# Turning v, r and a by rearranged DRAM copies and 32x32 blocks on VectorE in a fused RWKV-7 and MoE kernel

## The chip, the cores and the metric

The kernel runs on one core of a Trainium2 chip. The metric is device time in microseconds (us) for one execution; before the change it was 804.31 us, the median of 3 runs (802.88 to 806.55). The engines are named TensorE (PE in the profile, PEld for its weight loads), VectorE (DVE), ScalarE (ACT), POOL and SyncE (SP, whose queue is SPq). SyncE issues nearly all DMAs.

## The reference

Two blocks follow each other. The first is a recurrence over 768 steps, for 4 batches and 8 heads of 40 columns, with a 40x40 state per head:

```python
for t in range(S):
    kt, vt, rt = (k[:, :, t], v[:, :, t], r[:, :, t])
    wt, at, bt = (w[:, :, t], a[:, :, t], b[:, :, t])
    y[:, :, t] = np.einsum('bhd,bhde->bhe', rt, state)
    Sa = np.einsum('bhde,bhe->bhd', state, at)
    state_decay = state * wt[:, :, None, :] - np.einsum('bhd,bhe->bhde', Sa, bt)
    state = state_decay + np.einsum('bhd,bhe->bhde', vt, kt)
```

y is laid out as 3072 tokens of 320 columns, x, and the second block computes `h = x @ w_in; g = h * np.cos(h); out = g @ w_out` with d_ff = 2048. All of it is float32 on the chip; the MoE weights arrive as float64 words and are rounded there.

## The kernel before

**Chunks.** The sequence is cut into 24 chunks of C = 32 steps. A tile holds one chunk of one tensor with (batch, step) on the 128 partitions and (head, column) along the free side: 32 partitions a batch. Columns are padded from 40 to DP = 64 where pairs of heads are turned together. Each chunk's recurrence is rewritten as matrix products: Gram matrices between steps, a triangular inverse (made for four chunks at a time, mostly on VectorE), and the state carried from chunk to chunk.

**Turning.** These products need a tile's columns on the partitions. `turned` (L327) does it with four TensorE transposes of 128x128, each taking two heads: the result has (head parity, column up to 64) on the partitions and (pair of heads, batch, step) along the free side.
- v and r: `p2_in` (L584) copies the natural tiles nat_v and nat_r to the padded tiles vp and rp on POOL, with the heads reordered so that each transpose takes heads j and j + 4. `p2_v` (L604) turns both into one PSUM tile (eight transposes), and ScalarE copies the halves to vT and rT.
- a: `p1_a` (L406) works on two chunks at a time. From chunk 4 on it turns both (eight transposes), and `a_W` (L399) on VectorE multiplies the PSUM result by the cumulative decays wx into aT.
- w, k and b (scaled) are turned in the same way.

PSUM tiles for all of this come from `at` (L324), two in rotation.

**The recurrence of a chunk** is `ch_t`, `ch_q`, `ch_x`, `ch_s`, `ch_z` (states turned, products, result yt). `tokens` (L771) sends yt through a DRAM tile xd and back into xT, the MoE's input, 256 tokens for two chunks. The MoE is cut into pieces (`first_a`, `first_b`, `second`), 16 for each pair of chunks. A pair's pieces may begin with the chunk after the pair.

**Order.** The order is written out by hand at the end (from L1049): for each chunk a list of segments, with M where one MoE piece goes. The letters are t, q, x, s, z for the chain of chunk c; v, k, g for `p2_v`, `p2_k`, `p2_g` of chunk c + 1; pw, pa, pb, pn for w, a, b and the products of later chunks. `step` (L346) runs a segment; `later(n, work)` puts work, mostly loads, behind the n-th step from there. Every engine runs its instructions in this program order. Chunk 2 has 18 segments, chunk 3 has 25. `landed` (L597) has the next chunk's k, v and r loaded when both users of this one's have run. In the program the DMAs of SyncE use eight semaphores in turn, and each waits for the DMA eight places before it.

**Loads.** `load` (L146) fetches one tensor of a chunk with four DMAs, one for each batch, of 32 x 8 rows of 40 floats (160 bytes). `ws_fetch`, `ws_scan` and `ws_store` (L159 to L178) make the cumulative products of w, four chunks at a time, and keep them in a DRAM tile wd, from which w is loaded from chunk 4 on. During chunks 0 to 3 the same queue also fetches the MoE weights (words).

Of the kernel before, what the change touches and what calls it, by code (L numbers as in the profile page):

```python
# [9 lines left out]
F32 = mybir.dt.float32  # L10
I32 = mybir.dt.int32
U32 = mybir.dt.uint32
ALU = mybir.AluOpType
# [7 lines left out]
def kernel(  # L21
# [43 lines left out]
    nc = tc.nc  # L65
    B, H, S, D = r.shape
    P, C, DP = 128, 32, 64
    HH = H // 2
    NCH = S // C
# [5 lines left out]
    blk = [slice(C * i, C * i + C) for i in range(4)]  # L75
# [5 lines left out]
    ring = ctx.enter_context(tc.tile_pool(name="ring", bufs=7))  # L81
    sb1 = ctx.enter_context(tc.tile_pool(name="sb1", bufs=1))
    sb2 = ctx.enter_context(tc.tile_pool(name="sb2", bufs=2))
    sb3 = ctx.enter_context(tc.tile_pool(name="sb3", bufs=3))
    dram = ctx.enter_context(tc.tile_pool(name="dram", bufs=2, space=bass.MemoryType.DRAM))
# [4 lines left out]
    def kept(name, shape, n=1, fill=None, part=lambda t: t, on=nc.gpsimd):  # L90

        tiles = []
        for i in range(n):
            t = const.tile(shape, F32, tag=f"{name}{i}", name=f"{name}{i}")
            if fill is not None:
                on.memset(part(t), fill)
            tiles.append(t)
        return tiles
# [8 lines left out]
    src = {"r": r, "k": k, "v": v, "w": w, "a": a, "b": b}  # L107
# [11 lines left out]
    nat = {}  # L119
    for n, fill in (("w", 1.0), ("a", 0.0), ("b", 0.0)):  # L120
        for i in range(4):
            x = slice((i - 2) * H * DP, (i - 1) * H * DP)
            if i < 2:
                t = const.tile([P, H, DP], F32, tag=f"nat_{n}{i}", name=f"nat_{n}{i}")
            else:
                t = {
                    "w": w_in_sb[:, 0, late:], "a": w_in_sb[:, 1, late:], "b": late_out
                }[n][:, x].rearrange("p (h d) -> p h d", h=H)
# [4 lines left out]
    for n in "kvr":  # L133
        t = const.tile([P, H, D], F32, tag=f"nat_{n}", name=f"nat_{n}")
# [3 lines left out]
    vp, rp = (kept(n, [P, H, DP], 1, 0.0, padding, nc.vector)[0] for n in ("vp", "rp"))  # L138
# [4 lines left out]
    NZ = 2 * (C + DP) - DP + D  # L143
    qz = kept("qz", [P, B, 2, NZ], 1, 0.0, on=nc.vector)[0]

    def load(c, names, via=nc.sync, parts=range(B)):  # L146
        for n in names:
            for i in parts:
                at_c = src[n][i, :, c * C : (c + 1) * C, :]
                if n == "w" and c >= 4:  # L150
                    at_c = wd[c // 4][i, :, c % 4]
                via.dma_start(nat[n, c][blk[i], :, :D], at_c.rearrange("h t d -> t h d"))  # L152
# [171 lines left out]
    def at(name):  # L324
        return ps_a.tile([P, 2, 512], F32, tag="at", name=name)

    def turned(ps, x):  # L327

        for i in range(4):
            nc.tensor.transpose(  # L330
                ps[:, i * P : (i + 1) * P], x[:, 2 * i : 2 * i + 2].rearrange("p e d -> p (e d)"), ident
            )

    flat = lambda t: t.rearrange("p q t -> p (q t)")
    b4 = lambda t: t.rearrange("p (q t) -> p q t", t=C)
    unpad = lambda t: t[:, :, :D]
    G = {"rest": []}
# [5 lines left out]
    def later(steps, work):  # L343
        waiting.append([steps, work])

    def step(work, of_inv=0, of_w=0, small=False):  # L346


        before = list(waiting)
        work()  # L350
        G["small"] = small and G["kind"]
        for w in before:
            w[0] -= 1
            if w[0] == 0:
                waiting.remove(w)
                w[1]()
        for steps, n in ((inv_steps, of_inv), (w_steps, of_w)):
            for _ in range(min(n, len(steps))):
                steps.pop(0)()
# [29 lines left out]
    def from_one(c):  # L389

        nc.gpsimd.memset(G["wb", c][:, : 4 * P : C], 1.0)

    def over_w(c, wn):
        rw = ring.tile([P, H, D], F32, tag="rw", name="rw")
        nc.vector.reciprocal(rw, wn)  # L395
        nc.gpsimd.tensor_tensor(unpad(bn_b[c % 7]), unpad(nat["b", c]), rw, ALU.mult)  # L396
        G["rw", c] = rw

    def a_W(c, aps):  # L399
        aT = ring.tile([P, 4, P], F32, tag="aT", name="aT")  # L400
        nc.vector.tensor_tensor(
            aT.rearrange("p j (b t) -> p (j b) t", b=B), b4(aps), G["wx", c], ALU.mult
        )
        G["aT", c] = aT

    def p1_a(c):  # L406
        if c >= 4:
            ps = at("aps")
            for i in range(2):
                turned(ps[:, i], nat["a", c + i])  # L410
            for i in range(2):
                a_W(c + i, ps[:, i])
            over_w(c + 1, unpad(nat["w", c + 1]))
            return
        for c in range(c, c + 2):
            wn = ps_h.tile([P, 512], F32, tag="h", name="wn")
            aps = ps_o.tile([P, 512], F32, tag="o", name="aps")
            for j in range(4):
                nc.tensor.transpose(
                    wn[:, j * P : (j + 1) * P], G["wb", c][:, j * P + 1 : (j + 1) * P + 1], ident  # L420
                )
            from_one(c)
            turned(aps, nat["a", c])
            over_w(c, unpad(wn.rearrange("p (h d) -> p h d", h=H)))
            a_W(c, aps)
# [156 lines left out]


    def p2_in(c):  # L584
        for dst, m in ((vp, "v"), (rp, "r")):
            nc.gpsimd.tensor_copy(  # L586
                dst.rearrange("p (i f) d -> p f i d", f=2)[:, :, :, :D],
                nat[m, c].rearrange("p (f i) d -> p f i d", f=2),
            )
        landed(c)  # L590

    def p2_kn(c):
        nc.gpsimd.tensor_tensor(unpad(kn_b[c % 2]), nat["k", c], G["rw", c], ALU.mult)
        nc.gpsimd.tensor_copy(vvm[c % 2][:, :, C : C + D], nat["v", c])
        landed(c)

    def landed(c):  # L597

        G["users", c] = G.get(("users", c), 0) + 1
        if G["users", c] == 2 and c + 1 < NCH:  # L600
            for i, n in enumerate("kvr"):
                later(3 + i if c > 1 else 1, lambda n=n: load(c + 1, n))

    def p2_v(c):  # L604
        ps = at("vT")
        turned(ps[:, 0], vp)
        turned(ps[:, 1], rp)
        G["vT"] = sb3.tile([P, 4, P], F32, tag="opT", name="vT")
        G["rT", c] = sb2.tile([P, 4, P], F32, tag="rT", name="rT")
        nc.scalar.copy(G["vT"].rearrange("p j t -> p (j t)"), ps[:, 0])  # L610
        nc.scalar.copy(G["rT", c].rearrange("p j t -> p (j t)"), ps[:, 1])
# [38 lines left out]
    def ch_t(c):  # L650
        ps = at("sT")
        G["s"] = sb1.tile([P, 2 * B, P], F32, tag="s", name="s")
        for i in range(2 * B):
            nc.tensor.transpose(  # L654
                ps[:, i // 4, (i % 4) * P : (i % 4 + 1) * P], qz[:, i // 2, i % 2, C : C + P], ident
            )
        for i in range(2):
            nc.scalar.copy(G["s"][:, 4 * i : 4 * i + 4].rearrange("p i e -> p (i e)"), ps[:, i])  # L658

    def ch_q(c):  # L660
        ps = at("qps")
        for i in range(2 * B):
            for e in range(2):
                for f in range(2):
                    mm(
                        ps[half[e], f, i * C : (i + 1) * C], G["s"][half[f], i, half[e]],
                        G["rT", c][half[f], 2 * (i % 2) + e, blk[i // 2]], i == 0,
                    )
        for rows in half:
            nc.scalar.copy(  # L670
                pick(qz[rows], 0, (NZ - C, 2), (NZ, 2 * B), (1, C)),
                ps[rows, :, : 2 * B * C].rearrange("p f (i t) -> p f i t", t=C),
            )
# [247 lines left out]
    def main(c):  # L921
        def last():
            ch_z(c)
            if c + 2 < NCH:
                later(8 if c == 2 else 1, lambda: p2_kn(c + 2))

        return [lambda: ch_t(c), lambda: ch_q(c), lambda: ch_x(c), lambda: ch_s(c), last]

    with tc.manual_schedule():
# [64 lines left out]
        for seg in (other[1], *first[2:], *other[2:]):  # L994
            step(seg)
        scanned(1)
        p2_in(0)
        p2_kn(0)
        inv_space()
        inv_steps.extend(by_blocks(0))  # L1000
        v, k, g = p2(0)
# [44 lines left out]
        seconds = [lambda n=n: pair_second(0, n, n > 2) for n in range(4)]  # L1046
        (F1, F2, F3), (S1, S2, S3) = firsts[1:], seconds[1:]
        FILL = {(1, 6): 6, (1, 9): 14, (2, 0): 6, (2, 3): 6, (2, 5): 4, (2, 11): 29, (3, 3): 13, (3, 4): 20}
        for c in range(NCH):  # L1049
            t, q, x, s, z = main(c)  # L1050
            v, k, g = p2(c + 1) if c + 1 < NCH else [lambda: None] * 3
            q0 = c - c % 4 + 4
# [49 lines left out]
            n = len(segs)  # L1102
# [9 lines left out]
            for i, seg in enumerate(segs):  # L1112
                kept_busy(FILL.get((c, i), 0))
                while seg is s and ("rt", c) not in G:
# [57 lines left out]
```

## Time and profile before

| what | value |
|---|---|
| median of 3 runs | 804.31 us (802.88 to 806.55) |
| span of the profiled execution, first to last instruction | 803.7 us |
| what lies around the span, taken as median less span | 0.6 us |
| mean granted TensorE clock | 0.973 |
| DMA packets on SyncE's queue q1 | 177440, 52.11 MB |
| eight transposes of v and r (171.87 us in the chain) | 1.67 us |
| chunk 2 / 3 / 4 / 5 / 6 begins at | 90.8 / 127.5 / 169.9 / 206.5 / 245.0 us |

The profiled execution's own time is not listed apart from its span, so sums are made against the span and set beside the median. The profile lists busy time of each engine, the chain of work that ended last (each step followed back to what released it), groups of instructions with their mean duration, and each DMA queue with its packets. A chunk's place is told by the first transposes of the state (sT).

### The profile page before, as it was taken

The numbers are of one execution on the slowest core, as the hardware profiler recorded it, in microseconds if no ns is written. First come the engines' busy times: TensorE is split into PE (matmuls) and PEld (weight loads), VectorE is DVE, ScalarE is ACT, GpSimd is POOL, SyncE is SP. The second block draws the span as 40 slices with busy tenths as digits, with TensorE's granted clock in tenths as the row PEclk, the third lists the DMA queues.
The fourth block names the chain that finished last, engine by engine and source line by source line (L and its number), as shares of the span: only waits on it lengthen the run. The fifth ranks groups of instructions, "written<-read, shape, count | busy, mean of one in ns | idle before, by whom it ended". The sixth has DMA issues, their size and how long they took to land.

```text
span 803.7 us, 39602 instructions
## 1 busy us (share of the span) xinstructions
PE 753.0 (94%) x17812; PEld 578.6 (72%) x17812; DVE 487.9 (61%) x1025; ACT 387.2 (48%) x723; POOL 200.2 (25%) x354
## 2 busy tenths in 40 slices
PE   4777799999989999999999999999999999999997
PEld 4545577777767777777777787777787777777775
DVE  8879858854634796553895644994346863333231
ACT  1337766554434436545435635534645445354352
POOL 5326634320321220330330230332031122201000
PEclk9778999999999999999999999999999999999999
DMA  8675462443253324334224314223220222001000
GB/s 113 164 187 141 132 171 64 91 93 66 50 122 55 71 40 68 68 99 69 54 44 68 91 40 69 52 44 71 45 46 21 46 46 53 20 16 34 20 17 16
DMA packets 183304, 55.79 MB, mean 69 GB/s; under 512 B 157152, under 2 KB 178656, under 8 KB 183136
## 3 DMA queue, kind: packets, MB, share of 16 engines
q1 hardware_dynamic: 177440, 52.11, 30.1%
q8 instruction: 140, 2.29, 1.2%
q10 hardware_dynamic: 5440, 0.82, 0.7%
q0 software_dynamic: 256, 0.33, 0.3%
q14 instruction: 28, 0.23, 0.1%
HBM read 42.07 MB, written 11.14 MB: 66 GB/s over the span
## 4 chain that ended last, share of the span: by engine, by line
PE 68%; DVE 14%; ACT 5%; DMA 5%; issue 4%; POOL 2%; SPq 2%; DVEq 0%; ACTq 0%; POOLq 0%
PE ph L101 24%; PE po L101 20%; PE x0ps L101 4%; PE dps L101 3%; DVE rw L395 3%; PE gram L101 3%; PE vT L330 3%; PE sps L101 2%; DVE inv_tmp L494 2%; DVE inv L498 2%; PE nps L101 2%; PE qps L101 2%; PE sT L654 1%; SPq L152 1%; PE kT L330 1%
## 5 line engine op out<-in xcount | busy, mean ns | idle before, releaser
L101 PE MATMUL po<-w_out_sb,gT 128*128 128x320 f32 x768 | 223.3, 439 | 0.0
L101 PE MATMUL ph<-xT,w_in_sb 128*128 128x256 f32 x768 | 187.8, 389 | 1.9 <-issue 1.9
L101 PEld LDWEIGHTS po<-w_out_sb,gT 128*128 128x128 f32 x768 | 140.1, 190 | 54.4 <-issue 2.0
L101 PEld LDWEIGHTS ph<-xT,w_in_sb 128*128 128x128 f32 x768 | 140.8, 192 | 31.9 <-issue 14.1
L829 ACT ACTIVATE turns<-ph,rnd 128x512 f32<-128x512 f32 x96 | 64.2, 685 | 159.9 <-PE ph L101 159.5
L831 DVE SCALAR_TENSOR_TENSOR turns<-turns,ph 128x512 f32<-128x512 f32 x96 | 64.1, 683 | 115.3 <-ACT turns L829 115.0
L839 DVE TENSOR_TENSOR gT<-ph,turns 128x512 f32<-128x512 f32 x96 | 65.7, 686 | 39.1 <-ACT turns L836 39.1
L755 POOL TENSOR_TENSOR qz<-qz,wc 128x160 f32<-128x160 f32 x92 | 42.1, 475 | 167.5 <-DVE qz L754 166.8
L836 ACT ACTIVATE turns<-turns,half_pi 128x512 f32<-128x512 f32 x96 | 69.3, 722 | 3.1
L835 ACT ACTIVATE turns<-turns 128x512 f32<-128x512 f32 x96 | 60.2, 627 | 18.9 <-DVE turns L831 18.9
L101 PE MATMUL ph<-xT,w_in_tail 64*128 64x256 f32 (+1 forms) x512 | 55.0, 393 | 2.7 <-issue 2.7
L498 DVE TENSOR_TENSOR inv<-inv,inv_tmp 128x31 f32<-128x31 f32 (+15 forms) x124 | 50.7, 409 | 4.3
L754 DVE TENSOR_TENSOR qz<-dps,qz 128x160 f32<-128x160 f32 x92 | 28.9, 314 | 35.5 <-PE dps L101 35.4
L586 POOL COPY vp<-nat_v 128x320 f32<-128x320 f32 x24 | 12.0, 500 | 153.7 <-DMA nat_v<-in_v_dram 133.1
L494 DVE TENSOR_TENSOR inv_tmp<-u,inv 128x31 f32<-128x31 f32 (+15 forms) x124 | 48.3, 390 | 2.3
L395 DVE RECIPROCAL rw<-nat_w 128x320 f32<-128x320 f32 x20 | 42.8, 2141 | 0.1
L658 ACT COPY s<-sT 128x512 f32<-128x512 f32 x46 | 24.5, 583 | 35.9 <-PE sT L654 35.9
L101 PEld LDWEIGHTS ph<-xT,w_in_tail 64*128 64x128 f32 (+1 forms) x512 | 32.2, 160 | 12.2 <-issue 8.6
L766 POOL TENSOR_TENSOR yt<-yt,wb 128x512 f32<-128x512 f32 x24 | 31.6, 1316 | 22.3 <-DVE yt L761 22.3
L396 POOL TENSOR_TENSOR bn<-nat_b,rw 128x320 f32<-128x320 f32 x22 | 19.9, 906 | 43.9 <-DVE rw L395 37.1
L642 ACT COPY vvm<-gram 128x256 f32<-128x256 f32 x24 | 8.8, 368 | 45.6 <-DVE ag L637 45.2
L718 DVE TENSOR_TENSOR sm<-sps,su 128x128 f32<-128x128 f32 x48 | 11.7, 284 | 31.1 <-ACT sm L713 28.4
(136 smaller groups left out, 1130.6 us busy)
## 6 DMA issues: line engine op xcount, KB each, us to landing
words<-in_moe_w_in_dram SPq DMA_DIRECT2D x8, 512.0 KB
xd<-yt SPq DMA_DIRECT2D x48, 80.0 KB
out_dram<-ot SPq DMA_DIRECT2D x24, 160.0 KB
nat_k<-in_k_dram SPq DMA_DIRECT2D x92, 40.0 KB
nat_v<-in_v_dram SPq DMA_DIRECT2D x92, 40.0 KB
nat_r<-in_r_dram SPq DMA_DIRECT2D x92, 40.0 KB
nat_a<-in_a_dram SPq DMA_DIRECT2D x84, 40.0 KB
ws<-in_w_dram SPq DMA_DIRECT2D x5, 640.0 KB
```

The costliest lines, as they stand in the source:

```text
L101: nc.tensor.matmul(o, lhsT=lhsT, rhs=rhs, start=start, stop=stop, skip_group_check=True)
L330: nc.tensor.transpose(ps[:, i * P : (i + 1) * P], x[:, 2 * i : 2 * i + 2].rearrange("p e d -> p (e d)"), ident)
L395: nc.vector.reciprocal(rw, wn)
L494: nc.vector.tensor_tensor(tmp, u[:, j : j + 1, :j].to_broadcast([P, C - j, j]), x[:, j:, j : j + 1].to_broadcast([P, C - j, j]), ALU.mult,)
L498: nc.vector.tensor_tensor(x[:, j:, :j], x[:, j:, :j], tmp, ALU.subtract)
L755: nc.gpsimd.tensor_tensor(z, z, wc.rearrange("p (f m b) -> p f m b", f=2, m=2)[:, :, :, bb] .unsqueeze(3).to_broadcast([P, 2, 2, D]), ALU. ...
L766: nc.gpsimd.tensor_tensor(yt.rearrange("p j b t -> p (j b) t"), yt.rearrange("p j b t -> p (j b) t"), wx, ALU.mult)
L829: nc.scalar.activation(n, u, ACTF.Identity, bias=rnd, scale=1.0)
L831: nc.vector.scalar_tensor_tensor(n, n, -ROUND, u, ALU.add, ALU.subtract)
L835: nc.scalar.activation(n, n, ACTF.Abs)
L836: nc.scalar.activation(n, n, ACTF.Sin, bias=half_pi, scale=-2.0 * math.pi)
L839: nc.vector.tensor_tensor(gT[:, 2 * e : 2 * e + 2].rearrange("p f t -> p (f t)"), us[e], ns[e], ALU.mult)
```

## The change

v and r from chunk 6 on, and a from chunk 8 on, take another way.
- `spread` copies a range of chunks of one tensor from its DRAM input into a new DRAM tile, with one DMA for each head and each half of 32 columns: the tile's layout is [head group e, column half y, step, j, batch, 32 columns]. There are 16 copies for each of six ranges: a for chunks 8 to 12, v and r for 6 to 12, then v, r and a for 12 to 24. The second half reads columns 32 to 64, so it runs into the next step's row (those columns are not used); for the last head of the last range the last row is copied apart, to stay inside the tensor, which makes that copy 383 rows.
- The 96 copies wait in a list. `step` issues up to `G["rate"]` of them behind each segment: 2 in chunks 2 and 3, 1 from chunk 4 on.
- `load_turned` fetches a chunk with four DMAs of 32 rows of 2 KB: partitions then hold (e, y, step).
- `by_block` turns the tile with one VectorE instruction that transposes every 32x32 block. No PSUM tile is used. v and r go straight to vT and rT; a goes to aT and POOL multiplies it there by the decays.
- r is no longer loaded in the natural layout from chunk 6 on, a from chunk 8 on. v still is, since `p2_kn` copies it into vvm.

```diff
+    TURNED = {"v": 6, "r": 6, "a": 8}
+    apart, copies = {}, []
+
+    def spread(n, lo, hi):
+        x = src[n]
+        rows = (hi - lo) * C
+        to = dram.tile([2, 2, rows, HH, B, C], F32, tag=f"{n}t{lo}", name=f"{n}t")
+        for c in range(lo, hi):
+            apart[n, c] = to[:, :, (c - lo) * C : (c - lo + 1) * C]
+
+        def copy(h, y):
+            e, j = (h % 2, h // 2) if n == "a" else (h // HH, h % HH)
+            at = x.offset + h * S * D + lo * C * D
+            last = y == 1 and h == H - 1 and hi == NCH
+            parts = [(0, rows - last, 0, y * C, C)]
+            if last:
+                parts += [(rows - 1, rows, 0, C, D - C), (rows - 1, rows, D - C, 0, 2 * C - D)]
+            for r0, r1, o, d, m in parts:
+                nc.sync.dma_start(
+                    to[e, y, r0:r1, j, :, o : o + m],
+                    bass.AP(x.tensor, at + r0 * D + d, [[D, r1 - r0], [H * S * D, B], [1, m]]),
+                )
+
+        return [lambda h=h, y=y: copy(h, y) for h in range(H) for y in range(2)]
+
+    def load_turned(c, n, t):
+        for q in range(4):
+            nc.sync.dma_start(
+                t[blk[q]].rearrange("p h d -> p (h d)"),
+                apart[n, c][q // 2, q % 2].rearrange("t j b d -> t (j b d)"),
+            )
...
+    def by_block(to, x):
+        nc.vector.transpose(to.rearrange("p j t -> p (j t)"), x.rearrange("p h d -> p (h d)"))
...
         work()
+        for _ in range(min(G.get("rate", 0), len(copies))):
+            copies.pop(0)()
...
     def p1_a(c):
+        if c >= TURNED["a"]:
+            for i in range(2):
+                aT = ring.tile([P, 4, P], F32, tag="aT", name="aT")
+                by_block(aT, nat["a", c + i])
+                at_q = aT.rearrange("p j (b t) -> p (j b) t", b=B)
+                nc.gpsimd.tensor_tensor(at_q, at_q, G["wx", c + i], ALU.mult)
+                G["aT", c + i] = aT
+            over_w(c + 1, unpad(nat["w", c + 1]))
+            return
...
     def p2_in(c):
+        if c >= TURNED["v"]:
+            load_turned(c, "v", vp)
+            load_turned(c, "r", rp)
+            landed(c)
+            return
...
-            for i, n in enumerate("kvr"):
-                later(3 + i if c > 1 else 1, lambda n=n: load(c + 1, n))
+            for i, n in enumerate("kvr" if c + 1 < TURNED["v"] else "kv"):
+                later(3 + i if c > 1 else 1, lambda n=n: natural(c + 1, n))
...
     def p2_v(c):
+        if c >= TURNED["v"]:
+            G["vT"] = sb3.tile([P, 4, P], F32, tag="opT", name="vT")
+            G["rT", c] = sb2.tile([P, 4, P], F32, tag="rT", name="rT")
+            by_block(G["vT"], vp)
+            by_block(G["rT", c], rp)
+            return
...
+        for n, lo, hi in (
+            ("a", 8, 12), ("v", 6, 12), ("r", 6, 12), ("v", 12, NCH), ("r", 12, NCH), ("a", 12, NCH)
+        ):
+            copies.extend(spread(n, lo, hi))
         for c in range(NCH):
+            G["rate"] = {2: 2, 3: 2}.get(c, 1 if c > 3 else 0)
```

## The prediction

> **What bounds the kernel now.** I read the page's chain and engine table first, then busy time by stretch, then SyncE's own timeline and the chain around 170 us, because the change works through SyncE's queue.
>
> ```profile
> span 803.7 us, 39602 instructions
> PE 753.0 (94%) x17812; PEld 578.6 (72%) x17812; DVE 487.9 (61%) x1025; ACT 387.2 (48%) x723; POOL 200.2 (25%) x354
> ...
> PE 68%; DVE 14%; ACT 5%; DMA 5%; issue 4%; POOL 2%; SPq 2%; DVEq 0%; ACTq 0%; POOLq 0%
> ```
>
> TensorE carries 68% of the chain that ended last. By stretch (columns: length, PE, PEld, DVE, ACT, POOL busy, TensorE clock, DMA share, GB/s):
>
> ```profile
> 90.00:153.00 63.00, 58.66 (x1332) 45.41 (x1336) 49.77 (x85) 40.41 (x72) 27.16 (x37) 0.97 0.45 107
> 153.00:163.30 10.30, 10.01 (x334) 8.09 (x333) 6.12 (x13) 6.57 (x13) 5.59 (x9) 1.00 0.53 123
> 163.30:197.00 33.70, 31.96 (x949) 25.58 (x938) 18.09 (x46) 16.62 (x35) 2.62 (x7) 0.95 0.41 79
> 215.00:742.00 527.00, 518.36 (x12610) 402.06 (x12598) 308.55 (x683) 254.02 (x478) 114.49 (x208) 1.00 0.27 56
> ```
>
> From 215 to 742 us TensorE is busy 518 of 527 us: work taken from it there is time gained. But the copies go out between 90 and 197 us, where DMA is already 41 to 53% busy. There is no spare time there either: the chain around 146 us holds SyncE issuing a nat_a load and its landing, and at 173 us the MoE group of chunks 2 and 3 starts right after its input was fetched:
>
> ```profile
> 163.27 0.88 SPq L775 DMA_DIRECT2D xd<-yt  x2
> 169.09 0.39 SPq L785 DMA_DIRECT2D xT<-xd  x1
> 169.53 2.00 SPq L787 DMA_DIRECT2D xT<-xd  x2
> 171.63 2.77 SPq L152 DMA_DIRECT2D nat_w<-wd  x5
> ```
>
> xT's first part, issued at 169.1, lands about 2 us later; the group's first matmul runs at 173.4. Spare: some 2 us.
>
> **What is removed.** TensorE loses 18 x 8 transposes of v and r and 8 x 8 of a. Eight cost 1.67 us of the chain ("PE vT L330 x8" at 171.87). 18 x 1.67 + 8 x 1.67 = 43.5 us. ScalarE loses 36 copies of 0.59 us (21 us; it is 48% busy: worth nothing by itself). POOL loses 36 copies of 0.50 (18 us) and gains 16 multiplications like L766, 1.32 us each (21 us); at 25% busy that costs nothing, and a late aT would show first as a later inverse.
>
> VectorE gains 52 block transposes of 128x512. No row has one; L486 takes 1.24 us for 128x1024 contiguous, L502 1.95 with a stride, so half: 0.62 to 0.97. The operands are contiguous, I take 0.65. The 16 for a replace 16 L401 products of 0.67: even. The 36 for v and r are 23 us new. They hide where VectorE has room, but not in the inverse stages:
>
> ```profile
> 275.00:304.00 29.00, 28.23 (x637) 22.05 (x636) 27.83 (x56) 11.30 (x22) 9.31 (x17) 1.00 0.24 50
> 304.00:334.00 30.00, 29.41 (x758) 22.71 (x757) 16.13 (x39) 17.54 (x33) 5.14 (x9) 1.00 0.36 66
> ```
>
> In chunk 7 (275 to 304) VectorE is busy 27.8 of 29 us. Chunks 7, 11, 15 and 19 are alike, so I count no gain from one vT and one aps group in each: 4 x 3.34 = 13.4. Gain 43.5 - 13.4 = **30 us**; the bounds are 25 (less 8 transposes of 0.65 on those stages) and 43.5. In every fourth chunk the v transposes come two steps after the landing buffer vp is reloaded; VectorE waits there with the queue of MoE products behind it if the load is late. I put that at nothing, because SyncE reads it straight after xT; without that cover it is some 2 us a time, inside the bounds.
>
> **What is added: copies.** 96 rearranging copies, DRAM to DRAM, 128 bytes a packet: 32 of a (8 to 12) and v, r (6 to 12), 16 x 512 + 32 x 768 = 32768 packets, and 48 of chunks 12 to 24, 48 x 1536 = 73728 packets. All before had 177440 on this queue. In SyncE's program order they stand between 90 and 197 us of the old timeline. Removed loads come later and do not help there.
>
> How are packets shared among the 16 DMA engines? The page tells:
>
> ```profile
> q1 hardware_dynamic: 177440, 52.11, 30.1%
> ...
> q10 hardware_dynamic: 5440, 0.82, 0.7%
> ```
>
> The issues view gives SyncE's DMAs: 742. Their data packets, counted from the shapes (548 loads of 256, 48 stores xd of 160, and so on), are 166144, so 11296 of the 177440 are completions. 670 DMAs with 16 completions, the 48 of 40 rows with 10, and the 24 outputs whose outer size is 4 with 4 make 10720 + 480 + 96 = 11296 exactly; 16 for each would make 11872. So a DMA is cut evenly along its outer size, on as many engines (up to 16) as divide it. The copies have outer sizes 128, 192 and 384, hence 16 engines, except three: the last copy of v, r and a is cut to **383 rows**, to stay inside the tensor. 383 is prime: one engine, 1532 packets on it, where the others give 96. Whatever is issued later has a share behind them, and the program's waits hold SyncE too, since each DMA waits for the completion of the eighth before it.
>
> The Trainium skill ("DMA: Bandwidth & Descriptors", Why a DMA increments its semaphore by 16 and not by 1) states the same: the largest number up to 16 that divides the slowest dimension of both sides; 127 partitions go to one engine. The count here agrees for 10 and 4; no run here yet shows 1.
>
> Price of a packet, p. In the trace's DMA records a 160-byte load took 14 ns in the median, 15.9 in the mean; the q10 line gives 0.7% x 16 x 803.7 us / 5120 = 17.6 ns with completions. 512-byte packets, to and from DRAM, took 28. No row has a small write to DRAM. Bounds 14 and 28; I take **20 ns**, nearest to the 160-byte row with something for the second DRAM side.
>
> The skill's same page (Specifications) says that under 512 bytes a DMA does a read-modify-write. The trace has no DRAM write under 512 bytes. If that doubles 14 ns, p is 28 and the sum below ends at 988.
>
> **The sum**, on the busiest engine, at p = 20 (14; 28), with the places from TensorE's timeline of before:
> - 90 to 153 us. 2048 packets: 41 us. DMA is 45% busy, so 63 x 0.55 = 34.5 us are free. SyncE issues 48 more at 0.55 us (the mean of 72 there), 26 us, and had some 18 us in gaps of over 1 us: 8 late by that alone, 6.5 by the engines. The two partly add: lag 10 (8; 23).
> - Then to the group at 173.4: 27 copies of 96 and one of 1532, 4124 packets, 82.5 us; old DMA 5; less 10.3 that the old timeline had and 2 spare: 85 with the lag (58; 131).
> - To the w transposes of chunk 8 (194.0): 7 x 96 + 1532 = 2204, 44 us, old DMA 4, less TensorE's 20.6: 27.5 (14; 45).
> - To those of chunk 10 (237.9): 11 x 96 + 1532 = 2588, 52 us, old DMA 9, less 43.9: 17 (1; 38).
>
> TensorE waits 129.6 us (74; 214). 803.7 + 129.6 - 30 = 903.3. The median shown lies 0.6 above the span (launch and finish): **904**. Bounds 848 and 988.
>
> **Rivals.**
> - *The 383 rows are spread after all*, as if 384. Then 28 x 96 = 2688 packets up to 173.4, 56.5 us (38; 91), and the later stretches fit. 831 (813; 865). For: a lowering could regroup the shape. Against: 10 and 4 above.
> - *The copies hide* and the kernel is faster. DRAM copies would have to be as cheap as a 4-byte completion (9 ns in the records), on 16 engines: 8 + 24 + 5 - 12.3 = 25 us of wait against the full 43.5: 786. It decides below 11 ns a packet at a gain of 30, below 16 at 43.5. For: DMA is 70% idle over the whole span, TensorE bound for 500 us. Against: 106496 packets, 6656 an engine, in 107 us.
> - *Small DRAM writes are dear.* At 40 ns the same sum gives waits of 205, 72 and 69: 1120. For: no row excludes it. Against: the 512-byte store of xd costs no more than the load xT.
>
> **How the numbers follow.** Main case 0.62, spread 0.15, hidden 0.10, dear 0.13. Forecast 904. Leaving out the hidden and most of the dear case gives 812 to 1010. Faster by over 0.5% (about what a measurement of this kernel can tell from no change) 0.10, within 0.03, slower 0.87.
>
> **What would show it.** The new page's q1 line should hold some 258000 packets. DMA slices between 90 and 300 us: near 10 tenths first, then, in three runs of about 30 us, a sixteenth of that, with SyncE and TensorE idle. SyncE waits for vt, rt and at, TensorE waits at ph. From there on a group of four chunks is shorter by 6 to 8 us. No near-empty runs: the sharing is wrong. TensorE idle under 60 us before chunk 6: the price is wrong. Inverse stages longer than 29 us: VectorE costs more than I count.

## The result and the profile after

The changed kernel takes 926.93 us (median of 4 runs, 923.65 to 928.36), the kernel before beside it 804.32 (802.88 to 806.55): ratio 1.153, 95% interval 1.149 to 1.157. The forecast was 904, range 812 to 1010.

From the page of the changed kernel: totals, the slices (40 equal ones of 23.1 us, tenths), SyncE's DMA queue, and the shares of the chain:

```profile
span 924.4 us, 39331 instructions
...
PE 760.7 (82%) x17604; PEld 572.3 (62%) x17604; DVE 506.5 (55%) x1061; ACT 370.1 (40%) x687; POOL 203.6 (22%) x334
...
PE   5766976740187874998999989999899999999997
...
PEclk8788988875597877999999999999999999999999
DMA  8565677682837354424424144241432122201000
...
q1 hardware_dynamic: 258455, 73.82, 38.1%
...
PE 58%; SPq 16%; DMA 9%; DVE 7%; ACT 5%; issue 5%; POOL 1%; ACTq 0%; DVEq 0%; POOLq 0%
```

TensorE's share of the chain falls from 68 to 58%; SyncE's queue rises from 2 to 16%, DMA from 5 to 9%. The loss lies between 90 and 370 us: there are the low digits of PE, with a low clock under them, and one stretch in which TensorE does next to nothing (the digits 0 and 1, 208 to 254 us).

SyncE's timeline shows that stretch (columns: start, length, queue, line, what is copied, how many DMAs in a row):

```profile
200.25 24.95 SPq L166 DMA_DIRECT2D vt<-in_v_dram  x8
225.25 15.00 SPq L166 DMA_DIRECT2D rt<-in_r_dram  x12
...
248.44 19.84 SPq L166 DMA_DIRECT2D rt<-in_r_dram  x4
...
304.01 20.49 SPq L166 DMA_DIRECT2D at<-in_a_dram  x3
```

Twelve copies of r take 15 us, 1.25 each, but eight of v take 25, four of r 20 and three of a 20.5. In each of the last three rows one issue takes 18 to 19 us by itself. It is not that of the copy of 383 rows, which took 0.65 to 0.95 us, but that of the small end piece right behind it: there SyncE is held. By line (shortest, median, longest in ns):

```profile
L166 SPq DMA_DIRECT2D at<-in_a_dram x34: 557/634/19173, 92.3 to 323.9; - x34
L166 SPq DMA_DIRECT2D vt<-in_v_dram x34: 552/658/17950, 120.8 to 224.6; - x34
L166 SPq DMA_DIRECT2D rt<-in_r_dram x34: 557/660/17822, 143.7 to 267.7; - x34
```

What TensorE waited for between 170 and 370 us (total, times, longest):

```profile
PE ph L101 <- DMA xT<-xd: 58.0, 2, 46.1
```

The MoE's input xT, which stands behind these copies in SyncE's order, costs TensorE 58 us in two waits; before, no wait there was above 2.7 us. How much later than before TensorE comes to each place, in us (a chunk's place is its first state transposes):

| place | before | after | later by |
|---|---|---|---|
| chunk 3 | 127.5 | 136.1 | 8.6 |
| chunk 4 | 169.9 | 193.2 | 23.3 |
| MoE group of chunks 2, 3 | 173.4 | 249.7 | 76.3 |
| w transposes of chunk 8 | 194.0 | 275.5 | 81.5 |
| w transposes of chunk 10 | 237.9 | 336.9 | 99.0 |
| chunk 6 | 245.0 | 345.2 | 100.2 |
| next ph | 245.9 | 358.2 | 112.3 |
| chunk 8 | 304.2 | 414.7 | 110.5 |
| chunk 12 | 420.5 | 533.3 | 112.7 |
| chunk 16 | 536.8 | 649.4 | 112.6 |
| chunk 20 | 647.7 | 767.4 | 119.7 |
| end | 803.7 | 924.4 | 120.7 |

So 112 us are lost before 360 us, and of the expected gain nothing comes back: from chunk 8 to the end another 10 are lost.

### The profile page after: what moved, and what is told of

It is laid out like the page before. It is cut to its first block, busy times and chain, and to the rows that moved or that the text cites. A ratio compares the mean times of both kernels' runs of the same rounds, so it can differ in the third digit from the quotient of the medians.

```text
span 924.4 us, 39331 instructions
## 1 busy us (share of the span) xinstructions
PE 760.7 (82%) x17604; PEld 572.3 (62%) x17604; DVE 506.5 (55%) x1061; ACT 370.1 (40%) x687; POOL 203.6 (22%) x334
## 3 DMA queue, kind: packets, MB, share of 16 engines
q1 hardware_dynamic: 258455, 73.82, 38.1%
## 4 chain that ended last, share of the span: by engine, by line
PE 58%; SPq 16%; DMA 9%; DVE 7%; ACT 5%; issue 5%; POOL 1%; ACTq 0%; DVEq 0%; POOLq 0%
PE ph L101 22%; PE po L101 18%; SPq L166 9%; SPq L193 4%; PE x0ps L101 3%; PE dps L101 3%; PE gram L101 3%; DMA xd<-yt 2%; PE qps L101 2%; PE sps L101 2%; DVE inv L554 1%; PE nps L101 1%; DVE inv_tmp L550 1%; PE sT L721 1%; DMA words<-in_moe_w_in_dram 1%
## 5 line engine op out<-in xcount | busy, mean ns | idle before, releaser
L101 PE MATMUL ph<-xT,w_in_sb 128*128 128x256 f32 x768 | 194.8, 401 | 69.7 <-DMA xT<-xd 58.0
L101 PE MATMUL po<-w_out_sb,gT 128*128 128x320 f32 x768 | 233.5, 454 | 0.0
L101 PEld LDWEIGHTS ph<-xT,w_in_sb 128*128 128x128 f32 x768 | 146.0, 198 | 104.3 <-DMA xT<-xd 58.7
L101 PEld LDWEIGHTS po<-w_out_sb,gT 128*128 128x128 f32 x768 | 145.4, 197 | 58.6 <-issue 7.7
L737 ACT COPY qz<-qps 40x512 f32<-40x512 f32 x46 | 26.6, 579 | 61.8 <-PE qps L101 61.4
L101 PEld LDWEIGHTS <-idle 128*128 128x128 bf16 (+2 forms) x268 | 18.9, 101 | 20.8 <-issue 15.4
L489 ACT COPY bT<-bT 128x512 f32<-128x512 f32 x24 | 12.9, 589 | 45.7 <-PE bT L371 45.7
```

What stands on the lines that cost most here:

```text
L101: nc.tensor.matmul(o, lhsT=lhsT, rhs=rhs, start=start, stop=stop, skip_group_check=True)
```

## The experiments

**Theory.** The copies cost through three DMAs of 383 rows on one DMA engine each. *Rival:* the price is in the copies as such, whichever way they are shared out. A second question is why 26 fewer groups of transposes gained nothing. The first four kernels are compared with the kernel before at 800.05 us.

**e1_even.** The last copy cut into 368 and 15 rows:

```diff
-            parts = [(0, rows - last, 0, y * C, C)]
+            even = rows - 16 if last else rows
+            parts = [(0, even, 0, y * C, C)]
+            if last:
+                parts += [(even, rows - 1, 0, y * C, C)]
```

> The last copy of v, r and a is cut as 368 rows and 15 rows (16 x 23, and a divisor of its own), not as 383. Theory (a copy is shared by as many DMA engines as divide its outer size, 383 goes to one): the three issues of 17.95, 17.82 and 19.17 us that held SyncE fall to about 1.3 us, so the MoE group of chunks 2 and 3 starts some 17 us earlier than at 249.7, the w transposes of chunk 8 some 20 to 33 earlier, and the kernel takes 875 to 895 us instead of 927. Rival (the copies are slow by their number, the long issues are only where a full queue shows): the waits move to neighbouring issues and the time stays above 915 us.

878.48 us, 1.097 (1.094 to 1.100). The three long issues are gone (its lines by duration):

```profile
L169 SPq DMA_DIRECT2D at<-in_a_dram x35: 557/635/1693, 89.8 to 273.3; - x35
L169 SPq DMA_DIRECT2D vt<-in_v_dram x35: 552/673/1916, 118.1 to 205.6; - x35
L169 SPq DMA_DIRECT2D rt<-in_r_dram x35: 558/667/2248, 140.6 to 232.7; - x35
```

No issue is longer than 2.25 us, and 48 us of 123 are regained (45 by the ratios to the kernel before). The theory holds for these and falls for the rest: TensorE still waits 38.1 us for xT in two waits, the longer 30.6.

**e2_no_copies.** No copies; the blocks are loaded as rows of 2 KB from the inputs (other data in v, r and a):

```diff
-                apart[n, c][q // 2, q % 2].rearrange("t j b d -> t (j b d)"),
+                bass.AP(src[n].tensor, src[n].offset + ((c % 12) * 4 + q) * C * 512, [[512, C], [1, 512]]),
...
-            copies.extend(spread(n, lo, hi))
+            pass
```

> The 96 copies are left out; v, r and a from chunks 6 and 8 on are loaded with the same four DMAs of 32 rows of 2 KB straight from the inputs, so they hold other data. What remains is the late part alone: no transposes of v, r, a on TensorE, block transposes on VectorE. As predicted (TensorE bound, 30 us gained): 774 us. Theory formed from the profile after (VectorE is full in every fourth chunk, TensorE comes early to the next MoE piece, waits 3.5 us and then runs at a granted clock of 0.57 for some 4 us; net +10 us from chunk 8 to the end): 800 to 816 us, the same as before or slightly slower.

806.7 us, 1.007 (1.004 to 1.010). All the loss goes with the copies, but even with nothing to pay for them the new way of turning gains nothing. TensorE at the beginning of chunk 8, in this kernel's timeline:

```profile
296.12 1.04 PE L721 MATMUL sT<-ident,qz 128*128 128x128 f32 x8
300.63 3.22 PE L101 MATMUL ph<-xT,w_in_sb 128*128 128x256 f32 x8 [3.47 <-DVE gT L906]
```

TensorE stands 3.47 us until VectorE has made a gT (which frees the PSUM tile for ph). Chunks 12 and 16 begin with the same wait (3.47 and 3.44); before has none there. The eight ph matmuls that follow take 3.22 us; with a full clock they take 1.9.

**e3_vr_only, e4_a_only.** e2 with only v and r, or only a, turned the new way:

```diff
-    TURNED = {"v": 6, "r": 6, "a": 8}
+    TURNED = {"v": 6, "r": 6, "a": 24}
```

```diff
-    TURNED = {"v": 6, "r": 6, "a": 8}
+    TURNED = {"v": 24, "r": 24, "a": 8}
```

> As the kernel without copies, but a stays on TensorE in all chunks; only v and r (from chunk 6) are block-transposed, on other data. If VectorE's fullness in every fourth chunk decides, v and r bring all of VectorE's added 23 us and the wait stays: 798 to 815 us. If each TensorE transpose saved counts: 804 - 30 = 774 us.

798.74 us, 1.000 (0.997 to 1.003).

> As the kernel without copies, but v and r stay on TensorE in all chunks; only a (from chunk 8) is block-transposed, on other data. VectorE's load is then even (16 transposes of 0.69 us for 16 products of 0.67). If VectorE's load decides: half of the 8 groups of a, those outside the full stages, gain 1.67 us each, so 795 to 801 us. If each TensorE transpose saved counts: 804 - 13 = 791 us. If POOL's product (1.27 us each, in line before bn) delays the inverse: above 806 us.

806.28 us, 1.007 (1.004 to 1.009): not the gain I expected. Both parts were meant to gain; neither does, and a's loses by itself. The number fits the third way (POOL's product delays the inverse), but none of TensorE's waits behind chunk 8 is put down to POOL. What is new there are waits put down to "issue", in the middle of rows of small matmuls: 7.8 us in nine stops, the longest three 1.2 to 1.7 us in chunks 19 to 21, where before has none of 0.3 us or more.

**e5_pad.** Is that the place of the instructions in TensorE's program? e2 with more of the one-column matmuls that the kernel has ahead of chunk 19:

```diff
-        N_PAD = {0: 0, 19: 60}
+        N_PAD = {0: 0, 19: 108}
```

> As the kernel without copies (other data in v, r and a), but 108 instead of 60 tiny padding matmuls ahead of chunk 19. Up to there 176 transposes have gone; the page's 140 instruction packets of 16 KB for 2 x 17812 TensorE instructions give 256 instructions, 128 matmuls with their weight loads, a packet, and 176 - 128 = 48 brings the instructions of chunk 19 back to where they stood against these packets before the change. If the waits of 1.78 and 1.31 us inside sps of chunk 19 and gram of chunk 20 (none in the kernel before) come from where a packet ends: both vanish, the 48 cost 1.3 us, 802 to 806 us. If they come from anything that VectorE or a DMA does: they stay.

813.07 us in a single run (before 803.68). The wait of 1.78 us in chunk 19 became 0.84, that of 1.31 in chunk 20 is gone, and a new one of 0.88 stands in chunk 22; the whole did not become shorter. The stops move, but as a test of the total it is inconclusive.

**e6_off_full.** e2, with the new way only where the VectorE queue is not full: v and r in the third and fourth chunk of each four, a likewise from chunk 10 on (14 groups of transposes off TensorE instead of 26).

```diff
-    TURNED = {"v": 6, "r": 6, "a": 8}
+    TURNED = {"v": [c for c in range(6, NCH) if c % 4 > 1], "r": [c for c in range(6, NCH) if c % 4 > 1], "a": [c for c in range(8, NCH) if c % 4 > 1]}
...
-        if c >= TURNED["v"]:
+        if c in TURNED["v"]:
```

> No copies (other data), and block transposes only where VectorE has room: v and r of chunks 6, 7, 10, 11, ..., 22, 23 (executed one chunk earlier, so never in chunks 3, 7, 11, ... nor at the start of the next), a of the pairs 10, 14, 18, 22. That takes 14 groups of eight transposes off TensorE; a group of eight costs 0.89 us at full clock. If VectorE's fullness in every fourth chunk makes the wait of 3.5 us at the start of the next chunk and the low clock behind it: both are gone, 12.5 us less up to 7 us for new waits inside small matmuls, so 5 to 12 us below the kernel before. If the wait comes from something else in the new way (an early TensorE alone): it stays at its 3.5 us, and the time is 0 to 4 us below.

804.38 us against 803.68, 1.001 (0.999 to 1.003). All waits of 3.5 us are gone, which shows where they came from, but the 5 to 12 us did not follow. Chunk 11 is 33.2 us long (29.1 before) and chunk 20 30.2 (26.8), with new "issue" waits of 1.65 and 1.51 us.

**e9_same_count, e10_same_slots.** e6, with eight tiny matmuls in place of each removed group, so that TensorE's instructions keep their numbers; or with one, which keeps only the rotation of the PSUM tiles. Nothing else differs:

```diff
+            G["pad"](8)
...
+        G["pad"] = shifted
```

> As the kernel without copies and with block transposes only where VectorE has room (other data), but in the place of each of the 14 removed groups of eight transposes stand eight tiny matmuls of 26 ns, on a PSUM tile of their own in the same rotation. Every later TensorE instruction then stands at the number it had before the change. If the new waits inside small matmuls (1.65 us in chunk 11, 1.5 in chunk 20, each followed by some 5 us at a granted clock of 0.66 to 0.77) come from where the packets of 256 instructions end: they vanish, 14 x 0.89 - 14 x 0.21 = 9.5 us below the kernel before, 0.986 to 0.992. If it is TensorE's lead over VectorE or ScalarE that is lost elsewhere: 0.996 to 1.003.

> The same with one tiny matmul for each removed group: the PSUM rotation is that of the kernel before, the instruction numbers are not. If the rotation of the two PSUM tiles is what the eight tiny matmuls mended: as fast as those. If the instruction numbers are: waits of over 1 us inside small matmuls remain, 0.996 to 1.003.

Beside before at 800.12 us, e9 took 796.44, 0.996 (0.994 to 0.999), e10 804.14, 1.004 (1.002 to 1.006). The kernel with 98 more matmuls is 8 us faster. In e10 chunk 11 is 33.6 us long, in e9 29.4. TensorE inside chunk 11 of e10:

```profile
398.59 0.76 PE L101 MATMUL dps<-sm,bn 32*40 32x72 f32 x49
401.05 0.37 PE L101 MATMUL dps<-sm,bn 32*40 32x72 f32 x13 [1.71 <-issue]
```

It stops for 1.71 us between two matmuls of one row, with nothing named that it waits for; e9 has no stop of 0.7 us or more in that chunk. The traces tell what it waits for. Queue q8 brings packets of 16 KB, 140 in before, one for each 256 of TensorE's 35624 matmuls and weight loads (138 in the changed kernel, for 35208):

```profile
q8 instruction: 140, 2.29, 1.2%
```

All 14 traces together hold 179 "issue" waits of 0.7 us or more after their first 25 us. In 160 of them TensorE stands when 193 or 194 instructions of a block of 256 have started, and goes on 1.2 to 1.7 us after a packet of q8 has landed. (The other 19 are waits of ph at the start of a chunk, and two of aps in e3.) So these are waits for the next instructions, and matmuls put in or taken out ahead move the work that falls on such a place. From chunk 8 to the end, counted from 0.3 us up, before has none of them, e9 one of 0.8 us, e10 seven with 6.9 us, e2 six with 7.5, the changed kernel seven with 7.2. The gain of e9 is still below what I expected: chunks 9, 13 and 17 are 0.9 us shorter each, one group; the groups of a and of the fourth chunks gain half or nothing.

**e7_spread.** Real data again, and a version that might be faster: even cut, copies four chunks at a time and one in a step from chunk 3 on; v and r from chunk 8, a from chunk 12 (176 copies of 512 packets instead of 96 of up to 1536):

```diff
+        for n, lo, hi in [("v", 8, 12), ("r", 8, 12)] + [
+            (n, lo, lo + 4) for lo in range(12, NCH, 4) for n in "avr"
+        ]:
...
+            G["rate"] = int(c > 2)
```

> The copies as in the change, in their even form, but four chunks at a time and one behind each step from chunk 3 on: v and r from chunk 8, a from chunk 12; 176 copies of 512 packets (5.6 us of a DMA engine each 13 copies) in place of 96 larger ones. If it is the crowding of the copies into some 100 us that costs what is left after the even cut (878 us): 805 to 820 us. If each copy costs by itself, by SyncE's issue: 176 x 0.55 = 97 us of issue, 850 us and above.

882.62 us, 1.098 (1.095 to 1.101): wrong, it lies where the rival had it. The copies have 15% fewer packets, spread over more time, and it is not faster than e1.

**e8_selective.** e7 with e6's choice of chunks, two chunks at a time (v and r from 10, a from 14), 176 copies of 256 packets:

```diff
+        for n, lo, hi in [("v", 10, 12), ("r", 10, 12)] + [
+            (n, lo, lo + 2) for lo in range(14, NCH, 4) for n in "avr"
+        ]:
...
+            G["rate"] = int(c > 3)
```

> A version that computes the reference: copies for two chunks at a time, one behind each step from chunk 4 on, for v and r of chunks 10, 11, 14, 15, 18, 19, 22, 23 and a of 14, 15, 18, 19, 22, 23 only. 11 groups of transposes leave TensorE: 9.8 us. With copies hidden and VectorE not full: 3 to 9 us below the kernel before (0.989 to 0.996). If SyncE's 176 issues of 0.45 to 0.55 us delay the loads that come just in time: 1.0 to 1.02.

866.98 us, 1.078 (1.074 to 1.082), dearer than either expectation. The DMA engines have time now (40% busy from 127 to 212 us), but SyncE has hardly any:

```profile
196.67 0.56 SPq L169 DMA_DIRECT2D vt<-in_v_dram  x1
197.33 2.98 SPq L196 DMA_DIRECT2D nat_r<-in_r_dram  x4
200.36 1.88 SPq L169 DMA_DIRECT2D vt<-in_v_dram  x3
202.33 0.65 SPq L938 DMA_DIRECT2D out_dram<-ot  x1
203.03 1.26 SPq L169 DMA_DIRECT2D vt<-in_v_dram  x2
204.39 0.60 SPq L938 DMA_DIRECT2D out_dram<-ot  x1
```

Each start is nearly the end of the row above. From 171 to 330 us SyncE's gaps come to 6 us, and a DMA takes it 0.55 us in the median (0.3 to 1.9). TensorE waits at ph for 42.8 us in all, 34.1 of them put down to xT.

**e11_scalar_queue.** e8, its copies issued by ScalarE, and e9's tiny matmuls:

```diff
-                nc.sync.dma_start(
+                nc.scalar.dma_start(
```

> A version that computes the reference: the selective version with 176 small copies (867 us), but its copies are issued by ScalarE, and eight tiny matmuls stand for each removed group. If SyncE's queue in program order is what the copies cost (xT and the loads wait behind them): back to 795 to 812 us. If the copies' packets crowd the DMA engines: above 845 us. ScalarE's 176 issues of 0.5 us in line with its copies could cost up to the same: 820 to 845 us then.

814.88 us, 1.019 (1.016 to 1.022), between the two expectations. Same packets, same DMA engines: by the ratios, 47 of the 62 us that e8 lost against e6 are gone. The tiny matmuls can have 4 of them (e6 to e9; 7 by e10 to e9), so SyncE's order had some 40. The longest wait for xT is 1.5 us.

**e12_even_queue.** Does that repair the change itself? e1 with the same edit:

```diff
-                nc.sync.dma_start(
+                nc.scalar.dma_start(
```

> The change with its last copy cut evenly (368 + 15 rows, as in the run e1_even, 878.5 us) and all its copies given to DMA by ScalarE's queue instead of SyncE's. Every chunk and every value is as in the change. Queue theory: what is left of the copies' price after the even cut, 878.5 - 806.7 = 72 us, is mostly that loads, stores and xT stand behind copies in SyncE's issue; selective copies lost 867 - 815 = 52 us of 63 when they left that queue. Then 815 to 840 us, TensorE's waits for xT (30.6 and 7.4 us in e1_even) fall under 8 us in all, and SyncE has idle time again between 150 and 330 us. Rival, volume: the packets themselves (about 190000 of 13 ns, 155 us on each of 16 engines) hold up the loads whichever queue issues them; then 855 to 880 us with TensorE still waiting over 20 us for transfers before 330 us. A third way: ScalarE, which now waits in its own order until a copy can be issued, becomes late for its own arithmetic; then TensorE's waits are for ScalarE, and the time may be anywhere between.

851.62 us, 1.062 (1.056 to 1.068), before 802.52: by the ratios 28 of the 72 us are regained. Between the two again, by the third way. Busy time by stretch (length; PE, PEld, DVE, ACT, POOL; TensorE clock, DMA share, GB/s), first of e11, then of e12:

```profile
127.00:212.00 85.00, 79.92 (x2090) 63.30 (x2089) 60.73 (x119) 43.23 (x84) 26.14 (x45) 1.00 0.42 83
```

```profile
127.00:212.00 85.00, 57.19 (x1119) 43.85 (x1117) 38.87 (x70) 30.44 (x55) 21.02 (x35) 0.78 0.94 162
```

With all 96 large copies before chunk 6, DMA is 94% busy and TensorE does little more than half of its matmuls; with e11's smaller ones, spread out, 42%. And ScalarE, which now stands in its program order until a copy is issued, is late for its own work:

```profile
163.99 4.12 ACTq L169 DMA_DIRECT2D vt<-in_v_dram  x3
168.16 0.59 ACT L492 COPY bT<-bT 128x512 f32<-128x512 f32 x1 [4.28 <-DMA vt<-in_v_dram]
```

Such stops for copies come to 29.8 us on ScalarE from 134 to 210 us, and TensorE's longest waits in chunk 3 are now for ScalarE's noff, bT and kT (5.3 to 5.9 us each). How much is the volume and how much ScalarE's order was not taken apart. No version that computes the reference beats the kernel before; e11 comes nearest.

## Why the prediction was right, and where not

It was right in its sign and in the copies of 383 rows, and the total came within 2.5%, but partly by luck. Its terms were 73 us for the three copies (904 less the 831 of the rival), 56.5 for the even ones, and 30 gained; by the ratios the runs give 45, 72 (e1 to e2) and 6 lost (e2). Two errors in the wait went against each other, and the gain was wrong.

- **Sharing among engines: right.** Counted as in the prediction, the 258455 packets hold 13963 completions: 742 DMAs x 16 + 48 x 10 + 24 x 4, the 93 even copies x 16, the three of 383 rows x 1, the six end pieces x 4. Just 13963, and the trace holds as many packets of 4 bytes on this queue; e1, with 16 and 15 in place of each 1, holds 14053. So the 383 rows do go to one engine. This is the case of 1 that no run showed: the Trainium skill's rule ("DMA: Bandwidth & Descriptors", Why a DMA increments its semaphore by 16 and not by 1) agrees. e1 shows their price, 45 to 48 us. The rival "spread after all" is out.
- **Price of a packet: too high.** Taken at 20 ns; the copies' 128-byte packets took 13 ns in the median, 14.0 in the mean (in the same trace 14 and 16.1 for 160-byte loads). 1532 x 13 = 19.9 us, beside the held issues of 17.8 to 19.2. The skill's read-modify-write under 512 bytes (same page, Specifications) does not show as an extra over the loads of 160 bytes, and "small DRAM writes are dear" is out.
- **Lag of SyncE: too low.** 10 us were forecast at the end of the first part; TensorE came to chunk 4 23.3 late. I had priced 48 issues at 0.55 us, 26 in all, and let SyncE's gaps take up 18 of them. The gaps did: in the same work they shrank from 18.7 us to 2.3. But the 46 copies that came into it took 32 us, 0.69 each, and the other DMAs, with the short steps between all of them, some 5 more than before.
- **The places.** Up to the group of chunks 2 and 3: 85 forecast, 76.3 measured. To chunk 8's w: 27.5, and 5.2 (81.5 - 76.3). To chunk 10's: 17, and 17.5. From there to the ph of chunk 6, whose xT stands behind the last long copy, was not in the sum: 13.3, with a wait of 12.0 for xT. Together 129.6 forecast, 112 measured.
- **What failed in that sum** is that in its first part it counted DMA engines where SyncE's order counts. The slices "near 10 tenths" did not come: the engines were busy 69 and 60% (a row ends with clock, DMA share and GB/s):

```profile
90.00:153.00 63.00, 46.20 (x1071) 35.78 (x1056) 35.40 (x70) 33.14 (x59) 23.17 (x28) 0.89 0.69 143
153.00:176.60 23.60, 16.93 (x261) 12.86 (x262) 14.23 (x25) 8.57 (x16) 5.47 (x12) 0.86 0.60 94
```

  With 14 ns, near the packet that was measured, the sum gave 74 and not 112; the dear packet made up for the missing issue time. e8 and e11 show the queue by itself: some 40 us. Where large copies stand back to back the engines do set the pace: 1.25 us a copy (the row of twelve) is 96 packets of 13 ns. The three runs with few packets came too, one behind each copy of 383 rows: the slices with 2, 3 and 3 tenths.
- **The gain: wrong, 30 us forecast, 10 lost.** Three steps failed. *First* the size of a group: 1.67 us came from the chain at 171.87, where the granted clock was 0.54. In full clock the vT group at 422.15 of before ends at 423.05: 0.9 us. 26 groups are 23 us and not 43.5. *Second* the full stages. I took chunks 7, 11, 15 and 19 as worth nothing; the inverse stages did not become longer (chunk 11 took 27.2 us, 29.1 before), but VectorE's backlog came out in the chunk behind. First the clock of the 1.67 us and the beginning of chunk 12, both in before, then the changed kernel's TensorE at the beginning of chunk 12:

```profile
171.87:173.50 1.63, 1.63 (x9) 1.63 (x9) 1.46 (x6) 1.07 (x2) 0.00 (x0) 0.54 0.36 61
```

```profile
420.53 1.04 PE L654 MATMUL sT<-ident,qz 128*128 128x128 f32 x8
422.15 0.63 PE L330 MATMUL vT<-ident,vp 128*128 128x128 f32 x4 [0.58 <-DVE vvm L643]
422.61 0.60 PE L330 MATMUL vT<-ident,rp 128*128 128x128 f32 x4
423.05 1.89 PE L101 MATMUL ph<-xT,w_in_sb 128*128 128x256 f32 x8
```

```profile
524.76 1.89 PE L101 MATMUL ph<-xT,w_in_sb 128*128 128x256 f32 x8
...
533.27 1.04 PE L721 MATMUL sT<-ident,qz 128*128 128x128 f32 x8
537.90 3.11 PE L101 MATMUL ph<-xT,w_in_sb 128*128 128x256 f32 x8 [3.59 <-issue]
```

  It now stands for 3.59 us, and the same eight ph matmuls then take 3.11 us instead of 1.89, in low clock. Chunks 8, 12 and 16 are 5.8, 3.8 and 5.7 us longer; chunks 9, 13 and 17 give 1.3 to 1.7 back each. (The profile says "issue" here, gT in e2.) *Third*, the waits for instructions (e9 against e10, 8 us). From chunk 8 to the end TensorE's idle time rose from 9.3 to 25.7 us: three waits of 3.5 us, 10.5 in all, and seven stops for instructions, 7.2, where before has none. Its busy time fell by only 6.2 us, at a mean clock of 0.983 instead of 0.998. "A group of four chunks is shorter by 6 to 8 us" is refuted: chunks 8 to 12 took 118.6 us (116.3 before), 12 to 16 took 116.1 (116.3), 16 to 20 took 118.0 (110.9).
- **VectorE's price: right.** 0.65 us taken for a block transpose; by group (count, busy, mean ns, idle before):

```profile
L377 DVE STREAM_TRANSPOSE vT<-vp 128x512 f32<-128x512 f32 x18 | 12.6, 701 | 1.1 <-DMA vp<-vt 1.1
...
L377 DVE STREAM_TRANSPOSE rT<-rp 128x512 f32<-128x512 f32 x18 | 12.2, 676 | 2.0 <-DMA rp<-rt 2.0
```

  It waited 1.1 and 2.0 us for vp and rp in all: that load was covered, as I had it.
- **The rival "hidden", 786: wrong twice.** The packets were nearly as cheap as it asked (13 ns, against its bounds of 11 and 16), but neither the queue nor the gain went with it: e2, with no copies at all, is 0.7% slower than before.

The sum with what was measured: 803.7 + 112.3 of waits - 1.8 between there and chunk 8 + 10.2 after = 924.4.

## What to carry to other kernels

Before one row is cut off a DMA, factor what is left: three copies of 383 rows cost 45 to 48 us more than of 368 + 15. Price a DMA first by its issue, 0.55 to 0.7 us here for most, and by what stands behind it in its queue's program order, and then by its packets, which set the pace where large copies follow each other (1.25 us). Taking instructions out also moves the places where TensorE waits for its next ones. Take the price of a removed instruction from a row with full clock, and look for the cost of an added one on a full engine not in that stage but in the next, where its backlog meets the first instruction that needs it.

## What the runs showed of the hardware

- Behind a copy of 383 rows the next issue on its queue took 17.8 to 19.2 us; with the same rows as 368 + 15 none of the issues from there to the end pieces took over 1.25.
- 128-byte packets from DRAM to DRAM took no longer than 160-byte loads: 13 and 14 ns in the median.
- TensorE's clock after a stop: in e2 the 3.4 us behind the 3.47 us wait were granted 0.59; the 4.6 us ahead, most of them the wait, had 1.00. A wait of 3.5 us so costs about 1.3 us more. A shorter stop can do it too: in before a wait of 1.47 us ends at 168.90, and the clock from 170 to 171.87 was 0.50.
- 98 matmuls more made a kernel 8 us faster (e9, e10). TensorE's stops inside rows of matmuls come at one place in each 256 of its instructions and end 1.2 to 1.7 us after a packet of q8, 16 KB, has landed (160 waits in 14 traces).
- Which engine issues the copies was worth some 40 us (e8, e11). The Trainium skill ("DMA: Bandwidth & Descriptors", Issuing engines are not separate DMA queues) calls the time that a second issuing engine saves usually small relative to the DMA itself; here, with SyncE's gaps down to 6 of 159 us, it was not.
